# Cosine by way of whole turns: the turns found on VectorE from PSUM, and the quarter turn moved into the sine

## Chip, cores and metric

The kernel runs on one core of one Trainium2 chip. The metric is the device time of one execution in microseconds (us). A core has TensorE (PE: matrix products, into the memory PSUM), VectorE (DVE: elementwise), ScalarE (ACT: elementwise, and functions such as sine and exponential), GpSimd (POOL) and SyncE (SP: issues transfers). Each works through its own queue of instructions in order, and they wait for each other by semaphores.

## What is computed

Attention over a small memory (8 batches, 8 heads, 576 tokens, 64 numbers a head, 32 memory slots), and behind it a layer h -> h cos(h) between two large products:

```python
def _attn_ref(q, k, v, phi):
    a = np.exp(phi - np.max(phi, axis=2, keepdims=True))
    a = a / (np.sum(a, axis=2, keepdims=True) + 1e-09)
    k_m = np.einsum('bhsm,bhsd->bhmd', a, k)
    v_m = np.einsum('bhsm,bhsd->bhmd', a, v)
    scores = np.matmul(q, k_m.transpose(0, 1, 3, 2)) / np.sqrt(q.shape[-1])
    attn = softmax(scores)
    return np.matmul(attn, v_m)

def _moe_ref(x, w_in, w_out):      # x: 4608 x 512, w_in: 512 x 2048, w_out: 2048 x 512
    h = x @ w_in
    g = h * np.cos(h)
    return g @ w_out
```

(Here `softmax` is short for the written-out one of the reference.) The weights come as 64-bit floats.

## The kernel before

The 4608 tokens are taken in 12 **groups** of 384, and the 2048 hidden numbers in 16 chunks of 128; a **step** is one chunk of one group, so there are 192 steps. Two batches of 576 tokens make three groups. The middle one of each three (groups 1, 4, 7 and 10) holds the end of one batch and the start of the next, 192 tokens each, and its steps have two **regions** of 192 columns; all others have one region of 384 (`regions`). Group 0 works in float32, the others with every operand split in two float16 parts.

A step has these parts:

- `gemm1`: TensorE makes the tile `hp` (hidden numbers by tokens) in PSUM. v_m is folded into w_in beforehand (the tiles `vw`, or `vf` in group 0), so the softmaxed scores `aT` are its other operand: 6 matmuls of 384 columns, or 12 of 192 with two regions.
- `act`: `hp` is in a scaled unit, and `cu` (one column of 128 numbers, one for each batch) turns it into turns of the circle. ScalarE writes u = turns + 1/4 (L503, one instruction a region). VectorE converts u to the nearest integer into the space of `gp` (L508) and subtracts it (L509), so that u is within half a turn.
- `act_end`: ScalarE takes the sine of 2 pi u, which is cos(h) (L513). VectorE multiplies it by `hp` (L517); ScalarE makes the first float16 part of the product (L519), VectorE the second (L520), in `gp`. Group 0 has one product in float32 instead (L515).
- `gemm2`: 9 matmuls of 512 columns add the step's part of the outputs to three accumulators (L538; L533 in group 0). It runs four steps behind (`LAG`).

`hp` has three buffers in PSUM, `u` three and `gp` six in SBUF. A buffer of `hp` is free once L517 has read it.

Beside the steps other work is handed in piece by piece. Beside group 0: the weights are converted to float32 (L133 to L142) and folded for the first batch (L456, L458). Beside group 1: both weights are split in two float16 parts (L178, L179 for w_out; L189, L190 for w_in), as are the first batches' folded weights (L439, L440). From there on up to group 9 each next batch is prepared: the softmax over tokens and the sums over them, k_m and v_m, the scores and their softmax (`memory`, `attend`), and the fold of v_m into w_in (`fold`).

The program is written in this order; a scheduler then places the instructions in each engine's queue by priority and by its own estimate of when each one can run. Only where `keep_in_program_order` stands is a place kept. So a change of one instruction's engine can shift others.

Of the kernel before, what the change touches and what calls it, by code (L numbers as in the profile page):

```python
# [11 lines left out]
F32 = mybir.dt.float32  # L12
I16 = mybir.dt.int16
I32 = mybir.dt.int32
# [3 lines left out]
AF = mybir.ActivationFunctionType  # L18
ALU = mybir.AluOpType
# [26 lines left out]
def attention_then_ffn(ctx: ExitStack, tc: tile.TileContext, phi, phiT, kv, qT, w_in, w_out, out):  # L46
# [13 lines left out]
    make_identity(nc, ident)  # L60
    # in X, heads of even number hold [k | v] and those of odd number [v | k]
    vmask = const.tile([P, 2, 2], F32, name="vmask")
# [4 lines left out]
    w_in_sb = const.tile([P, NP, DF], F32, name="w_in_sb")  # L67
    # w_out: block f + 1 holds rows f * 128 on as float32, later block f their two float16 parts
    wo = const.tile([P, NF + 1, DM], F32, name="wo")

    def wo_parts(f):
        return wo[:, f].bitcast(F16).rearrange("p (w e) -> p w e", w=2)

    vl = const.tile([P, NP, 2, M], F16, name="vl")
    nc.vector.memset(vl, 0.0)
# [24 lines left out]

# [1 line left out]
    raws = itertools.count()  # L102
# [4 lines left out]
    def load_w_in(j):  # L107
        if j in (2, 3):
            # the space of w_out's last blocks, which come later
            t = wo[:, 13:17] if j == 2 else wo[:, 9:13]  # L110
            t = t.bitcast(I32).rearrange("p c (f t) -> p c f t", t=2)
        else:
            t = ld.tile([P, NP, WS, 2], I32, tag=next_raw(), name=f"raw_in_{j}")
        nc.sync.dma_start(out=t, in_=w_in[:, 2 * WS * j:2 * WS * (j + 1)].rearrange("(c p) (f t) -> p c f t", p=P, t=2))
        loads["in", j] = t
# [8 lines left out]
    def to_float32(dst, raw, sq_to, pin=False):  # L124
        # the upper half of dst gets the sign, the lower half the last three bits of the mantissa,
        # which lead the low word. The high word as a float32 times 2^-112 has the exponent less
        # 896, three bits too low, and nothing above it.
        low, high = raw[:, :, :, 0], raw[:, :, :, 1]
        flat = raw.rearrange("p c f t -> p c (f t)")
        halves = dst.bitcast(I16).rearrange("p c (f t) -> p c f t", t=2)  # L130
        low_top = flat.bitcast(U8).rearrange("p c (f t) -> p c f t", t=8)[:, :, :, 3]
        high_top = flat.bitcast(I8).rearrange("p c (f t) -> p c f t", t=8)[:, :, :, 7]
        begin = (nc.vector.tensor_scalar(out=halves[:, :, :, 1], in0=high_top, scalar1=0.0, scalar2=-32768.0,  # L133
                                         op0=ALU.is_lt, op1=ALU.mult),
                 nc.scalar.activation(halves[:, :, :, 0], low_top, AF.Copy, scale=2.0 ** -5, bias=-31.0 / 64.0))
        if pin:
            for ins in begin:
                tc.keep_in_program_order(ins)
        nc.scalar.activation(high.bitcast(F32), high.bitcast(F32), AF.Copy, scale=2.0 ** -112)
        nc.vector.scalar_tensor_tensor(out=dst.bitcast(I32), in0=high, scalar=3, in1=dst.bitcast(I32),  # L140
                                       op0=ALU.logical_shift_left, op1=ALU.bitwise_or)
        nc.scalar.activation(low.bitcast(F32), dst, AF.Square, accum_out=sq_to)  # L142
# [6 lines left out]

    # e, a power of two, with every magnitude below 2 e; and 2^14 / e  # L150
    def power_of_two(dst, src):
# [10 lines left out]
    def weight_scale(kind, name):  # L162
        # halving the exponent of the largest sum of squares
        m = const.tile([P, 1], F32, name=f"m_{name}")
        nc.vector.tensor_reduce(out=m, in_=sq[:, kind], op=ALU.max, axis=AX.X)
        nc.gpsimd.partition_all_reduce(m, m, channels=P, reduce_op=RED.max)
        nc.vector.tensor_scalar(out=m, in0=m, scalar1=2.0, scalar2=2.0 ** -100, op0=ALU.mult, op1=ALU.max)
        nc.vector.tensor_scalar(out=m.bitcast(I32), in0=m.bitcast(I32), scalar1=1, scalar2=None,
                                op0=ALU.logical_shift_right)
        nc.vector.tensor_scalar(out=m, in0=m, scalar1=2.0 ** 63, scalar2=None, op0=ALU.mult)  # L170
        e = const.tile([P, 1], F32, name=f"e_{name}")
        power_of_two(e, m)
        st["e", name] = e
        st["s", name] = to_range(f"s_{name}", const, f"s_{name}", e)
# [6 lines left out]

    # w_in in two float16 parts. A head's 64 rows of both parts are brought together on the 128
    # partitions, so that one pass takes both: the first part stays where it is, the second goes to
    # the other half. The slices are kept where a load or an earlier slice was.
    def w_in_split(q, c):
# [17 lines left out]

    # the maximum over the tokens, on all partitions, far ahead of its use
    def maximum(b):
# [7 lines left out]

# [1 line left out]
    def memory(b):  # L215
        a = loads.pop(("phi", b))
        if b < NT:
            # by the tensor engine, from phi transposed
            nmx = wk.tile([P, 2], F32, tag="nmx", name=f"nmx_{b}", bufs=1)
            nc.vector.tensor_reduce(out=nmx, in_=loads.pop(("phiT", b)), op=ALU.max, axis=AX.X)  # L220
            top = small_ps(f"top_{b}")[:, 0:HM]
            for g in range(2):
                nc.tensor.matmul(top[:, g * P:(g + 1) * P], lhsT=nmx[:, g:g + 1].broadcast_to([P, P]), rhs=ident,
                                 start=True, stop=True)
        else:
            top = st["top", b]
# [4 lines left out]
        for c0, c1, n in ((0, 2, P), (2, 4, P), (4, 5, S - 512)) if b == 0 else ((0, 4, P), (4, 5, S - 512)):  # L231
# [3 lines left out]
            if b >= NT:  # L235
                # not sooner: the maximum takes its time
                tc.keep_in_program_order(ins)
# [54 lines left out]

    # the powers of two that bring the two-part float16 operands into range
    def v_scale(b):
# [4 lines left out]
    def scales(b):  # L299
# [10 lines left out]
        else:  # L310
            # the first part of v_m for both parts of w_in, the second part for the first one alone
            sv = to_range(f"sv_{b}", wk, "sv", st["ev", b])
# [9 lines left out]

    # attention over the memory: scores with (head, memory) on the partitions; 32 by 32 blocks are
    # transposed for the softmax over a head's memory, and back
    def attend(b):
        qt, km = loads.pop(("q", b)), st["km", b]
        flat = wk.tile([P, 4 * S], F16, tag="aT", name=f"aT_{b}", bufs=3)
        # the first group works in float32, on the first GT tokens of the first batch
        t32 = GT if b == 0 else 0
# [90 lines left out]

    # v_m folded into w_in
    def fold_psum(b, q, g):
# [46 lines left out]

# [1 line left out]
    def regions(grp):  # L471
# [26 lines left out]

    def act(grp, f, hp, pin=False):
        u = ew.tile([P, GT], F32, tag="u", name=f"u_{grp}_{f}", bufs=3)  # L500
        gp = ew.tile([P, GT], F32, tag="gp", name=f"gp_{grp}_{f}", bufs=6)
        for b, t0, c0, n in regions(grp):
            ins = nc.scalar.activation(u[:, c0:c0 + n], hp[:, c0:c0 + n], AF.Copy,  # L503
                                       scale=st["cu", b] if grp else 1.0 / (2.0 * math.pi), bias=0.25)
            if pin:
                tc.keep_in_program_order(ins)
        ni = gp.bitcast(I32)
        nc.vector.tensor_copy(out=ni, in_=u)  # L508
        nc.vector.tensor_tensor(out=u, in0=u, in1=ni, op=ALU.subtract)  # L509
        return u, gp  # L510

    def act_end(grp, f, hp, u, gp):
        nc.scalar.activation(u, u, AF.Sin, scale=TWO_PI_BELOW)  # L513
        if grp == 0:
# [10 lines left out]
    def gemm2(grp, f, gp):  # L525
        if f == 0:
            # nothing else is left for the small tiles' banks beside the last group
            spare = 2 if grp == 11 else 0
# [11 lines left out]
        if f == NF - 1:  # L540
            # the last group waits for the third accumulator of the one before alone
            for t in (2,) if grp == 10 else range(3):
                evacuate(grp, t)
# [24 lines left out]

# [1 line left out]
    load_phi(0)  # L570
# [31 lines left out]
    fold_first(1)  # L602
    # the other weights, in the order in which they are needed, each a step of the first group
    todo = [("out", 0)]
# [48 lines left out]
    for i in range(12 * NF):  # L653
# [16 lines left out]
        begun.append((grp, f, hp, *act(grp, f, hp, last)))  # L670
        # with nothing else between them, a step's first half goes before the second half of the one before
        while len(begun) > (grp >= 9):
# [66 lines left out]
```

## Time and profile before

| | |
|---|---|
| median of 3 runs | 719.68 us (718.75 to 721.45) |
| span of the profiled execution, first to last instruction | 718.0 us |
| granted TensorE clock, mean over the span | 0.993 |
| TensorE's matmuls L538 (second product) | 1584, 371.3 us busy |
| TensorE's matmuls L494 (first product) | 1440, 202.9 us busy |
| ScalarE's L503, L513, L519 | 118.4 + 99.9 + 89.2 us busy |
| VectorE's L508, L509, L517, L520 | 67.4 + 105.8 + 96.9 + 96.6 us busy |

The profile is of one execution. It has for each instruction its engine, start and length, its line and the tiles that it writes and reads ("u<-hp,cu" writes u and reads hp and cu), and, for idle time, what ended it. An instruction's length runs on until its last result is written, and the next one on the same engine can start a little before. The chain of work that ended last goes back from the last instruction, at each step to what released it. A row of a stretch holds, after its bounds and length, each engine's busy time with the number of its instructions, the granted clock, and the share and rate of the transfers.

### The profile page before, as it was taken

What the parts mean: (1) busy time and instruction counts of PE and PEld (TensorE: products, weight loads), DVE (VectorE), ACT (ScalarE), POOL (GpSimd) and SP (SyncE); (2) the same over time, 40 slices, a digit from 0 to 9 for tenths busy, and PEclk for the clock granted to TensorE, in tenths of its full rate; (3) what the DMA queues carried; (4) which work ended last, traced back from release to release, by engine and by line L of the source; (5) the groups of instructions that cost most, each with busy time, mean ns of one, the idle gap of its engine ahead of it and who ended that gap; (6) DMA issues with size and microseconds to landing.
All of it is one profiled execution on the core that took longest, in us unless ns stands there. A gap on an engine that the chain in (4) does not pass through costs nothing.

```text
span 718.0 us, 12024 instructions
## 1 busy us (share of the span) xinstructions
PE 694.5 (97%) x4578; PEld 357.3 (50%) x4578; DVE 569.6 (79%) x1257; ACT 520.3 (72%) x964; POOL 14.6 (2%) x36
## 2 busy tenths in 40 slices
PE   6689999999999999999999999999999999999997
PEld 2345444565454444565444444566444544555553
DVE  2779999998988997589877897669776987676763
ACT  1699999889886875678756685668767785665553
POOL 0000000000000000000000100000000000000000
PEclk9799999999999999999999999999999999999999
DMA  9994981526405300152104310152100000100101
GB/s 282 382 326 159 310 306 30 132 60 188 148 8 160 110 1 1 45 166 67 45 1 135 96 48 1 45 168 67 44 1 1 22 25 1 45 1 1 45 0 45
DMA packets 31417, 66.72 MB, mean 93 GB/s; under 512 B 2176, under 2 KB 10880, under 8 KB 31360
## 3 DMA queue, kind: packets, MB, share of 16 engines
q1 hardware_dynamic: 27040, 58.09, 25.5%
q10 hardware_dynamic: 4320, 7.87, 2.9%
q8 instruction: 36, 0.59, 0.3%
q14 instruction: 21, 0.17, 0.1%
HBM read 52.31 MB, written 9.44 MB: 86 GB/s over the span
## 4 chain that ended last, share of the span: by engine, by line
PE 59%; DVE 20%; ACT 14%; issue 3%; DMA 3%; POOL 0%; SPq 0%; DVEq 0%; ACTq 0%; POOLq 0%
PE acc L538 34%; PE hp L494 18%; PE pv L433 3%; DVE u L517 3%; DVE gp L520 2%; DVE u L509 2%; DMA phi<-in_phi 2%; ACT u L513 2%; DVE gp L508 2%; ACT L513 1%; DVE vw L440 1%; PE psA L248 1%; ACT raw_out L142 1%; DVE wo L179 1%; PE sc L350 1%
## 5 line engine op out<-in xcount | busy, mean ns | idle before, releaser
L538 PE MATMUL acc<-wo,gp 128*128 128x512 f16 x1584 | 371.3, 379 | 0.0
L538 PEld LDWEIGHTS <-gp 128*128 128x128 f16 x1584 | 153.4, 98 | 161.6 <-issue 2.6
L494 PE MATMUL hp<-aT,vw 128*128 128x192 f16 (+1 forms) x1440 | 202.9, 284 | 1.4 <-DVE u L517 1.2
L494 PEld LDWEIGHTS <-vw 128*128 128x128 f16 x1440 | 125.0, 98 | 84.0 <-issue 30.7
L513 ACT ACTIVATE u<-u 128x384 f32<-128x384 f32 x192 | 99.9, 524 | 88.5 <-DVE u L509 87.4
L517 DVE SCALAR_TENSOR_TENSOR u<-hp,u 128x384 f32<-128x384 f32 x176 | 96.9, 553 | 45.8 <-ACT u L513 43.5
L503 ACT ACTIVATE u<-hp,cu 128x192 f32<-128x192 f32 (+1 forms) x240 | 110.9, 492 | 17.0 <-PE hp L494 10.8
L520 DVE TENSOR_TENSOR gp<-u,gp 128x384 f16<-128x384 f32 x176 | 96.6, 552 | 29.8 <-ACT gp L519 29.3
L519 ACT CAST gp<-u 128x384 f16<-128x384 f32 x176 | 89.2, 509 | 40.0 <-DVE u L517 37.9
L509 DVE TENSOR_TENSOR u<-u,gp 128x384 f32<-128x384 f32 x192 | 105.8, 552 | 3.1
L508 DVE CAST gp<-u 128x384 int32<-128x384 f32 x192 | 67.4, 354 | 20.4 <-ACT u L503 18.7
L533 PE MATMUL acc<-wo,gp 128*128 128x512 f32 x96 | 45.5, 599 | 0.2 <-DVE gp L515 0.2
L440 DVE SCALAR_TENSOR_TENSOR vw<-pv,vw 128x512 f16<-128x512 f32 x48 | 33.1, 689 | 4.7 <-ACT vw L439 3.4
L439 ACT ACTIVATE vw<-pv 128x512 f16<-128x512 f32 x48 | 28.3, 591 | 6.4 <-PE pv L433 5.5
L485 PE MATMUL hp<-aT,vf 128*128 128x384 f32 x64 | 26.4, 545 | 4.2 <-DVE gp L515 2.0
L513 ACT ACT_TABLE_LOAD x23 | 29.5, 1283 | 0.4
L533 PEld LDWEIGHTS acc<-wo,gp 128*128 128x128 f32 x96 | 17.2, 190 | 17.4 <-issue 12.9
L248 PE MATMUL psA<-kv,phi 128*32 128x129 f32 (+1 forms) x640 | 23.5, 277 | 0.8 <-ACT phi L238 0.8
L554 ACT ACTIVATE ob<-acc,os 128x512 f32<-128x512 f32 x28 | 18.5, 683 | 8.0 <-PE acc L538 6.1
L248 PEld LDWEIGHTS psA<-kv,phi 128*32 128x32 f32 (+1 forms) x640 | 16.0, 109 | 11.2 <-issue 5.9
L485 PEld LDWEIGHTS hp<-aT,vf 128*128 128x128 f32 x64 | 12.4, 206 | 17.2 <-issue 5.3
L350 PE MATMUL sc<-q,km 128*64 128x256 f32 (+3 forms) x192 | 20.2, 336 | 0.0
(129 smaller groups left out, 553.3 us busy)
## 6 DMA issues: line engine op xcount, KB each, us to landing
kv<-in_kv SPq DMA_DIRECT2D x32, 516.0 KB, 5.8
q<-in_qT SPq DMA_DIRECT2D x8, 1152.0 KB, 5.7
raw_out<-in_w_out SPq DMA_DIRECT2D x8, 1024.0 KB, 5.5
out<-ob ACTq DMA_DIRECT2D x30, 256.0 KB, 2.1
raw_in<-in_w_in SPq DMA_DIRECT2D x6, 1024.0 KB, 7.3
phi<-in_phi SPq DMA_DIRECT2D x8, 512.0 KB, 6.7
w_in_sb<-w_in_parts SPq DMA_DIRECT2D x12, 256.0 KB, 4.6
phiT<-in_phiT SPq DMA_DIRECT2D x4, 576.0 KB, 8.0
```

The lines of the kernel that those rows point to most:

```text
L248: nc.tensor.matmul(psA[32 * j:32 * (j + 1), g * KV:(g + 1) * KV], lhsT=a[:n, c, h * M:(h + 1) * M], rhs=kvs[c][:n, h * KV:(h + 1) * KV], s ...
L440: nc.vector.scalar_tensor_tensor(out=vw[:, 1, g], in0=src, scalar=T, in1=vw[:, 0, g], op0=ALU.mult, op1=ALU.subtract)
L494: nc.tensor.matmul(hp[:, c0:c0 + n], lhsT=vw[:, wi, g, fo * P:(fo + 1) * P], rhs=aT[:, ai, g, c1:c1 + n], start=(k == 0), stop=(k == 5))
L503: ins = nc.scalar.activation(u[:, c0:c0 + n], hp[:, c0:c0 + n], AF.Copy, scale=st["cu", b] if grp else 1.0 / (2.0 * math.pi), bias=0.25)
L508: nc.vector.tensor_copy(out=ni, in_=u)
L509: nc.vector.tensor_tensor(out=u, in0=u, in1=ni, op=ALU.subtract)
L513: nc.scalar.activation(u, u, AF.Sin, scale=TWO_PI_BELOW)
L517: nc.vector.scalar_tensor_tensor(out=u, in0=hp[:, :GT], scalar=2.0 ** -17, in1=u, op0=ALU.mult, op1=ALU.mult)
L519: nc.scalar.copy(gp[:, 0], u)
L520: nc.vector.tensor_tensor(out=gp[:, 1], in0=u, in1=gp[:, 0], op=ALU.subtract)
L533: nc.tensor.matmul(accs[grp][t], lhsT=gp[:, t * P:(t + 1) * P], rhs=wo[:, f + 1], start=(f == 0), stop=(f == NF - 1))
L538: nc.tensor.matmul(accs[grp][t], lhsT=gp[:, gi, t * P:(t + 1) * P], rhs=parts[:, wi], start=(f == 0 and gi == 0 and wi == 0), stop=(f == N ...
```

## The change

`act` no longer uses ScalarE. VectorE takes `hp` from PSUM, multiplies it by the turns' scale, adds 1/4 and writes the result as integers into `gp`, one tensor_scalar a region. Then one scalar_tensor_tensor a region multiplies `hp` by the same scale and subtracts the integers. What is left is u without its quarter turn, and the sine gets that back as a bias, from a constant column `quarter` that is set once. All else of a step is as before.

```diff
+    quarter = const.tile([P, 1], F32, name="quarter")
+    nc.vector.memset(quarter, TWO_PI_BELOW / 4.0)
...
     def act(grp, f, hp, pin=False):
         u = ew.tile([P, GT], F32, tag="u", name=f"u_{grp}_{f}", bufs=3)
         gp = ew.tile([P, GT], F32, tag="gp", name=f"gp_{grp}_{f}", bufs=6)
+        ni = gp.bitcast(I32)
         for b, t0, c0, n in regions(grp):
-            ins = nc.scalar.activation(u[:, c0:c0 + n], hp[:, c0:c0 + n], AF.Copy,
-                                       scale=st["cu", b] if grp else 1.0 / (2.0 * math.pi), bias=0.25)
+            turns = st["cu", b] if grp else 1.0 / (2.0 * math.pi)
+            ins = nc.vector.tensor_scalar(out=ni[:, c0:c0 + n], in0=hp[:, c0:c0 + n], scalar1=turns, scalar2=0.25,
+                                          op0=ALU.mult, op1=ALU.add)
             if pin:
                 tc.keep_in_program_order(ins)
-        ni = gp.bitcast(I32)
-        nc.vector.tensor_copy(out=ni, in_=u)
-        nc.vector.tensor_tensor(out=u, in0=u, in1=ni, op=ALU.subtract)
+        for b, t0, c0, n in regions(grp):
+            turns = st["cu", b] if grp else 1.0 / (2.0 * math.pi)
+            nc.vector.scalar_tensor_tensor(out=u[:, c0:c0 + n], in0=hp[:, c0:c0 + n], scalar=turns,
+                                           in1=ni[:, c0:c0 + n], op0=ALU.mult, op1=ALU.subtract)
         return u, gp

     def act_end(grp, f, hp, u, gp):
-        nc.scalar.activation(u, u, AF.Sin, scale=TWO_PI_BELOW)
+        nc.scalar.activation(u, u, AF.Sin, scale=TWO_PI_BELOW, bias=quarter)
```

The new lines shift the numbers: in the changed kernel the tensor_scalar is L508 and the scalar_tensor_tensor L514, the sine is L519, the product L523, and the two halves are L525 and L526; the weight splits L179 and L190 are L181 and L192, and L440 is L442. In the rows below a name's first number is the step's chunk, the last one the tile's.

VectorE's queue in group 1, before, from the third step's conversion to the same step's last half:

```order
L508 CAST gp_3_987<-u_3_986 128x384
L509 TENSOR_TENSOR u_3_986<-u_3_986,gp_3_987 128x384
L508 CAST gp_4_1021<-u_4_1020 128x384
L509 TENSOR_TENSOR u_4_1020<-u_4_1020,gp_4_1021 128x384
L517 SCALAR_TENSOR_TENSOR u_3_986<-hp_3_961,u_3_986 128x384
L508 CAST gp_5_1060<-u_5_1059 128x384
L440 SCALAR_TENSOR_TENSOR vw_2_996<-pv_2_1_1078,T_750,vw_2_996 128x512
L520 TENSOR_TENSOR gp_3_987<-u_3_986,gp_3_987 128x384
```

The same queue and step in the changed kernel:

```order
L508 TENSOR_SCALAR gp_3_973<-hp_3_947,cu_702 128x192
L508 TENSOR_SCALAR gp_3_973<-hp_3_947,cu_738 128x192
L526 TENSOR_TENSOR gp_2_926<-u_2_925,gp_2_926 128x384
L514 SCALAR_TENSOR_TENSOR u_3_972<-hp_3_947,cu_702,gp_3_973 128x192
L514 SCALAR_TENSOR_TENSOR u_3_972<-hp_3_947,cu_738,gp_3_973 128x192
L442 SCALAR_TENSOR_TENSOR vw_2_982<-pv_2_0_983,T_740,vw_2_982 128x512
L523 SCALAR_TENSOR_TENSOR u_3_972<-hp_3_947,u_3_972 128x384
L181 SCALAR_TENSOR_TENSOR wo<-wo,s_out 128x512
L526 TENSOR_TENSOR gp_3_973<-u_3_972,gp_3_973 128x384
```

Two instructions of 384 columns have become four of 192. Steps 4 and 5 no longer stand between the third step's parts; the weights' splits and folds do, and they are still in this stage.

ScalarE's queue at the same place, before:

```order
L503 ACTIVATE u_3_986<-hp_3_961,cu_710 128x192
L503 ACTIVATE u_3_986<-hp_3_961,cu_748 128x192
L503 ACTIVATE u_4_1020<-hp_4_1007,cu_710 128x192
L503 ACTIVATE u_4_1020<-hp_4_1007,cu_748 128x192
L503 ACTIVATE u_5_1059<-hp_5_1046,cu_710 128x192
L503 ACTIVATE u_5_1059<-hp_5_1046,cu_748 128x192
L513 ACTIVATE u_3_986<-u_3_986 128x384
```

And in the changed kernel:

```order
L519 ACTIVATE u_3_972<-u_3_972,quarter 128x384
L525 CAST gp_3_973<-u_3_972 128x384
L441 ACTIVATE vw_2_982<-pv_2_1_1064,T_740 128x512
L180 ACTIVATE wo<-wo,s_out 128x512
L191 ACTIVATE w_in_parts_1158<-w_in_sb,s_in 128x512
L519 ACTIVATE u_4_1006<-u_4_1006,quarter 128x384
```

The copies are gone, and the sines stand among the weights' splits.

VectorE's queue in group 11, the last, before:

```order
L508 CAST gp_11_7293<-u_11_7292 128x384
L509 TENSOR_TENSOR u_11_7292<-u_11_7292,gp_11_7293 128x384
L517 SCALAR_TENSOR_TENSOR u_11_7292<-hp_11_7285,u_11_7292 128x384
L520 TENSOR_TENSOR gp_11_7293<-u_11_7292,gp_11_7293 128x384
L508 CAST gp_12_7318<-u_12_7317 128x384
```

And in the changed kernel:

```order
L508 TENSOR_SCALAR gp_11_7172<-hp_11_7164,cu_6135 128x384
L526 TENSOR_TENSOR gp_10_7148<-u_10_7147,gp_10_7148 128x384
L514 SCALAR_TENSOR_TENSOR u_11_7171<-hp_11_7164,cu_6135,gp_11_7172 128x384
L523 SCALAR_TENSOR_TENSOR u_11_7171<-hp_11_7164,u_11_7171 128x384
L508 TENSOR_SCALAR gp_12_7196<-hp_12_7188,cu_6135 128x384
```

The second half of a step now stands behind the next step's tensor_scalar.

## Prediction, made before the changed kernel ran

> **What bounds the kernel now.** I read the head of the page first, for the busy shares, then the chain of work that ended last, stretch by stretch, and then the busy time of the engines in the same stretches.
>
> ```profile
> span 718.0 us, 12024 instructions
> PE 694.5 (97%) x4578; PEld 357.3 (50%) x4578; DVE 569.6 (79%) x1257; ACT 520.3 (72%) x964; POOL 14.6 (2%) x36
> ```
>
> A TensorE that is busy for 97% of the span looks like the one bound, but matmul ends are modelled, and the share is a mean over stages. The chain of a late stretch shows what a step costs when nothing holds it up:
>
> ```profile
> 664.33 1.94 PE acc L538 x9
> 666.27 0.97 PE hp L494 x6
> 667.25 1.94 PE acc L538 x9
> ```
>
> Nine matmuls of the second product (1.94 us) and six of the first (0.97) follow each other without a gap: 2.92 us a step, TensorE alone on the chain. The next two rows are the chain's shares by line in 109 to 167 us (group 1) and in 282 to 338 us (group 4):
>
> ```profile
> by line: DVE wo L179 14.6%; DVE w_in_parts L190 13.6%; DVE vw L440 12.7%; DVE u L509 11.9%; DVE gp L520 10.2%; DVE u L517 10.0%; DVE gp L508 7.3%; DMA w_in<-w_in_parts 6.7%; issue 2.4%; ACT L238 2.2%; ACT raw_out L142 2.1%; ACT u L503 1.8%;
> ...
> by line: PE acc L538 20.8%; PE hp L494 13.0%; DMA phi<-in_phi 12.3%; DVE u L517 4.5%; ACT u L513 3.7%; DVE u L509 3.7%; DVE gp L520 3.5%; PE pv L433 2.9%; DVE gp L508 2.8%; DVE at L352 2.8%; DVE rs L361 2.5%; ACT phi L238 2.4%; DVE rm L356
> ```
>
> In the first stretch the seven VectorE lines make 80% of the chain. In the second TensorE leads. So the kernel has two parts, and the busy times of the stretches say where the border lies. The stretches are, in order: group 0, 1, 2 and 3 of the twelve groups of 16 steps, and group 10:
>
> ```profile
> 32.20:109.30 77.10, 73.68 (x325) 35.38 (x326) 69.93 (x141) 75.44 (x109) 1.59 (x5) 0.96 0.81 273
> 109.30:166.60 57.30, 57.02 (x350) 31.63 (x349) 56.90 (x120) 52.70 (x113) 0.66 (x2) 1.00 0.29 70
> 166.60:226.40 59.80, 58.88 (x458) 29.26 (x457) 51.50 (x123) 50.83 (x84) 0.97 (x3) 1.00 0.46 142
> 226.40:281.80 55.40, 54.96 (x336) 25.59 (x333) 48.90 (x112) 39.58 (x76) 2.06 (x4) 1.00 0.15 46
> 607.20:657.40 50.20, 50.20 (x378) 30.14 (x377) 32.76 (x66) 29.53 (x69) 0.00 (x0) 1.00 0.05 17
> ```
>
> Each row gives the stretch, its length, and the busy time of TensorE, its weight loads, VectorE, ScalarE and GpSimd. In group 0 ScalarE is busy for 75.44 of 77.10 us. In **group 1 VectorE is busy for 56.90 of 57.30 us**: nothing can be added to it there for free. From group 3 on VectorE has some 6 us of room in a group, in group 10 over 17.
>
> **The change, part by part.** It takes one ScalarE copy per region from each step, and the SBUF conversion and subtraction from VectorE. It adds, per region, a tensor_scalar from PSUM to int32 and a scalar_tensor_tensor from PSUM and int32. Steps of groups 1, 4, 7 and 10 have two regions of 192 columns, the others one of 384. The rows of what goes, and of the nearest kin of what comes:
>
> ```profile
> L503 ACT ACTIVATE u<-hp,cu 128x384 f32<-128x384 f32 x112 | 63.8, 576 | 12.4 <-PE hp L494 8.0 <-ACT ob L554 1.7 <-DVE gp L520 0.6
> L503 ACT ACTIVATE u<-hp,cu 128x192 f32<-128x192 f32 x128 | 47.3, 419 | 4.6 <-PE hp L494 2.9 <-ACT ob L554 1.2 <-DVE gp L520 0.2
> L503 ACT ACTIVATE u<-hp 128x384 f32<-128x384 f32 x16 | 7.5, 492 | 0.1
> L508 DVE CAST gp<-u 128x384 int32<-128x384 f32 x192 | 67.4, 354 | 20.4 <-ACT u L503 18.7
> L509 DVE TENSOR_TENSOR u<-u,gp 128x384 f32<-128x384 f32 x192 | 105.8, 552 | 3.1
> L517 DVE SCALAR_TENSOR_TENSOR u<-hp,u 128x384 f32<-128x384 f32 x176 | 96.9, 553 | 45.8 <-ACT u L513 43.5
> L440 DVE SCALAR_TENSOR_TENSOR vw<-pv,vw 128x512 f16<-128x512 f32 x48 | 33.1, 689 | 4.7 <-ACT vw L439 3.4
> L440 DVE SCALAR_TENSOR_TENSOR vw<-pv,T,vw 128x512 f16<-128x512 f32 x8 | 5.9, 744 | 0.1
> L262 DVE TENSOR_SCALAR X<-psA,den 128x128 f32<-128x128 f32 x16 | 5.3, 344 | 0.2
> L552 DVE TENSOR_SCALAR ob<-acc,os 128x512 f32<-128x512 f32 x1 | 0.8, 750 | 3.8 <-PE acc L538 3.8
> ```
>
> *The tensor_scalar.* No row before writes int32 from PSUM. L262 and L552 are tensor_scalars from PSUM with a scalar taken from a column, 344 ns at 128 columns and 750 at 512. That is 406 / 384 = 1.06 ns a column, so 344 + 256 x 1.06 = 615 ns at 384 columns and 412 at 192. The lower bound is the conversion that goes, 354 ns at 384 columns, which reads SBUF and writes the same int32. I take 615, as it reads PSUM. The Trainium skill, "VectorE: DVE Perf Modes", section "Why PSUM operands drop a tier", says that fp32 from PSUM has no doubled mode since PSUM offers VectorE one read port. By it the cheap conversion is lost, and 615 would stand; the trace agrees in that the PSUM rows run at 1.06 ns a column, while 354 ns for 384 columns is less than that.
>
> *The scalar_tensor_tensor.* L517, with PSUM and SBUF inputs, takes 553 ns at 384 columns, and L440 689 at 512: again 1.06 a column, so 553 - 204 = 349 at 192. A scalar from a column costs 744 - 689 = 55 more, so 608 and 404. Group 0 has its scalar in the instruction: 560 and 553.
>
> *What VectorE is held for* is less than a duration, since the next one starts before the end:
>
> ```profile
> 134.24 0.36 DVE L508 CAST gp<-u 128x384 int32<-128x384 f32 x1
> 134.64 0.56 DVE L509 TENSOR_TENSOR u<-u,gp 128x384 f32<-128x384 f32 x1
> 135.11 0.35 DVE L508 CAST gp<-u 128x384 int32<-128x384 f32 x1
> ...
> 136.44 0.35 DVE L508 CAST gp<-u 128x384 int32<-128x384 f32 x1
> 136.71 0.74 DVE L440 SCALAR_TENSOR_TENSOR vw<-pv,T,vw 128x512 f16<-128x512 f32 x1
> ```
>
> The subtraction's 0.56 us hold it for 0.47 (134.64 to 135.11), so 0.09 overlap. The conversion holds it for 0.40 us before its own subtraction and 0.27 before other work. The pair costs 0.74 to 0.87 us, 0.80 in the middle. After the change a two-region step costs 2 x (0.412 - 0.09) + 2 x (0.404 - 0.09) = 1.27 us, **0.47 more** (0.40 to 0.53); the second tensor_scalar fills the first one's wait. A one-region step costs 0.525 + 0.52, with up to 0.1 of wait 1.10, so 0.30 more; in group 0 some 0.16 more.
>
> *Group 1*: 16 x 0.47 = **7.5 us**. VectorE is full there, and the order keeps that stage's other VectorE work (the weight splits L179 and L190, the folds L440) in it. So all of it counts.
>
> *Group 0*: ScalarE loses 14 copies of 0.49 us in the stretch (6.9), and VectorE gains 16 x 0.16 = 2.6, to 72.5 of 77.10. The sine's bias from a column makes each sine longer; by L503 with and without its column that is 576 - 492 = 84 ns, 1.2 us here. With both engines near full, and each waiting for the other, I take **-1 us**, from 0 to -2.9 (72.5 plus the 1.7 us that ScalarE now idles).
>
> *Groups 2 to 9.* A group of one-region steps gets 16 x 0.30 = 4.8 us of VectorE, which fits as a mean: 48.90 + 4.8 in 55.40. It doesn't fit in the bursts in which a batch is prepared:
>
> ```profile
> 240.00:264.00 24.00, 24.00 (x143) 10.92 (x142) 22.90 (x49) 20.35 (x39) 0.00 (x0) 1.00 0.22 82
> 312.00:336.00 24.00, 24.00 (x182) 14.47 (x181) 22.91 (x61) 17.45 (x39) 2.05 (x4) 1.00 0.33 107
> 408.00:432.00 24.00, 24.00 (x129) 11.61 (x128) 23.25 (x52) 20.86 (x36) 0.25 (x1) 1.00 0.27 83
> ```
>
> Each stretch of 24 us has some 7 steps, so 7 x 0.30 = 2.1 us more (7 x 0.47 = 3.3 in the second, which is in group 4): 25.0, 26.2 and 25.3 against 24.0, an excess of 4.5 us. The steps in hand (three product tiles, and four steps between the two products) take up part, so I count **3.7 us**, from 0 to 4.5.
>
> *Groups 10 and 11*: nothing. VectorE goes from 32.76 to at most 41 of 50.20. At the end the chain of a step on VectorE (tensor_scalar, last step's subtraction of halves, scalar_tensor_tensor, sine, product) is about 2.9 us, as long as TensorE's 2.92; should it lag, 54 matmuls of the second product stand ready behind it:
>
> ```profile
> 702.25 11.67 PE acc L538 x54
> ```
>
> *The rest*: the column of quarter turns is one small memset early on. The copies gone, the sines' table loads fall by two and the exponentials' by two in the order, on ScalarE only, which has room from group 2 on. Buffers keep their lives: the product tile was held until L517 reads it, and still is. The DMA queue of SyncE has the same transfers; a few of k and v come sooner among the weights' loads, which I cost at nothing, as no load is on the chain of groups 0 and 1 but the 3.89 us of w_in's parts.
>
> *Sum*: 718.0 - 1 + 7.5 + 3.7 = 728.2 us of span. The median of the runs is 719.68, 1.7 above the span, so 729.9: **730 us, 1.4% slower**.
>
> **The rivals.** *Spare time absorbs it (not slower).* Over groups 0 to 2 VectorE is busy for 69.93 + 56.90 + 51.50 = 178.3 of 194.2 us and gets 2.6 + 7.5 + 4.8 = 14.9, to 193.2. Were it never idle, with ScalarE relieved, group 2 would win back what group 1 loses; TensorE isn't on top in group 2 either. The mechanism decides if group 2 shrinks from 59.8 to about 54. With the bursts hidden too, and group 0 at -2.9, that gives 717 to 720, and 715 if ScalarE's relief takes 2 us more from group 2. Against it: the order leaves group 1's VectorE work in group 1, and group 2 itself gets 4.8 us more. Chance 0.18 (0.05 faster, 0.13 the same).
>
> *VectorE becomes the bound in every preparing stage (slower still).* Groups 2 to 9 get 6 x 4.8 + 2 x 7.5 = 43.8 us. Were it to count in the half of the steps beside which a batch is prepared, that is 22 us in place of 3.7, so 748. For it: VectorE now also waits for the sine right behind its own work in each step. Against it: TensorE leads there, with several us of VectorE free. Chance 0.13.
>
> *The int32 comes out of PSUM as quickly as out of SBUF.* Then group 1 adds 16 x (0.95 - 0.80) = 2.4 us, the bursts nothing: 721. Chance 0.07 (0.05 the same, 0.02 slower). By the skill's rule above it can't be; that sentence changes nothing in the 0.07, which comes from the missing row.
>
> **How the numbers follow.** My forecast gets 0.57, and lies between 724 and 742. A new order that gains or loses elsewhere keeps 0.05 (0.03 faster, 0.02 slower). About 0.5% is what a measurement of this kernel can tell from no change. Faster by over that: 0.05 + 0.03 = 0.08. The same: 0.13 + 0.05 = 0.18. Slower: 0.57 + 0.13 + 0.02 + 0.02 = 0.74. The range goes from 717 to 748: it leaves out the lower part of the first rival and the upper half of the second.
>
> **What would show it.** Right: tensor_scalars of about 412 and 615 ns, scalar_tensor_tensors of 404 and 608; group 1 some 65 us long with VectorE over 98% busy; ScalarE's busy time down by 63.8 + 47.3 + 7.5 less 192 x 0.084, about 102 us; group 10 as long as before. Wrong: group 1 under 60 us, or groups 3 to 9 longer by over 2 us each, or group 0 shorter by over 3.

## The result: 1.55% slower, and the profile after

| | before | after |
|---|---|---|
| median | 719.21 us | 730.76 us |
| ratio, 95% interval | | 1.0155 [1.0137, 1.0173] |
| span of the profiled execution | 718.0 us | 728.0 us |

A second time, on another chip, the changed kernel took 730.74 us against 720.61: 1.0136 [1.0114, 1.0159].

The head of the changed kernel's page:

```profile
span 728.0 us, 11891 instructions
PE 695.7 (96%) x4578; PEld 358.6 (49%) x4578; DVE 631.0 (87%) x1385; ACT 432.3 (59%) x705; POOL 13.5 (2%) x36
```

VectorE has 61.4 us more, ScalarE 88.0 less, TensorE about the same (1.2 more). The groups of instructions that are new, and the sine with its bias (line, engine, shapes, count, then busy time and the mean in ns):

```profile
L514 DVE SCALAR_TENSOR_TENSOR u<-hp,cu,gp 128x384 f32<-128x384 f32 x112 | 68.0, 609 | 0.7
L508 DVE TENSOR_SCALAR gp<-hp,cu 128x384 int32<-128x384 f32 x112 | 67.4, 604 | 3.7 <-PE hp L496 3.4
L508 DVE TENSOR_SCALAR gp<-hp,cu 128x192 int32<-128x192 f32 x128 | 48.0, 408 | 4.9 <-PE hp L496 4.5
L514 DVE SCALAR_TENSOR_TENSOR u<-hp,cu,gp 128x192 f32<-128x192 f32 x128 | 47.2, 407 | 0.0
L508 DVE TENSOR_SCALAR gp<-hp 128x384 int32<-128x384 f32 x16 | 8.7, 550 | 2.2 <-PE hp L487 2.2
...
L519 ACT ACTIVATE u<-u,quarter 128x384 f32<-128x384 f32 x192 | 116.9, 613 | 172.0 <-DVE u L514 155.4 <-DVE l L286 6.4 <-DVE ev L154 3.9
```

Where the 10 us lie is seen by group. These are the changed kernel's stretches for groups 0, 1, 2 and 3, and group 10, with the columns as before (bounds, length, busy TensorE, weight loads, VectorE, ScalarE, GpSimd, granted clock, share and rate of the transfers):

```profile
32.40:112.40 80.00, 76.11 (x324) 35.74 (x324) 71.64 (x139) 74.22 (x99) 1.64 (x5) 0.94 0.74 252
112.40:177.40 65.00, 58.40 (x355) 32.18 (x355) 64.01 (x145) 44.10 (x75) 0.66 (x2) 1.00 0.24 61
177.40:237.30 59.90, 56.88 (x451) 29.59 (x450) 58.13 (x128) 39.77 (x64) 0.98 (x3) 1.00 0.45 143
237.30:292.80 55.50, 55.09 (x337) 25.66 (x334) 52.22 (x113) 32.93 (x58) 2.07 (x4) 1.00 0.17 56
617.20:667.40 50.20, 50.20 (x377) 30.13 (x376) 41.28 (x102) 22.70 (x41) 0.00 (x0) 1.00 0.05 17
```

Group 1 is 7.7 us longer by these rows (57.30 to 65.00), group 0 2.9 (77.10 to 80.00), and groups 2, 3 and 10 are as long as before within 0.3. In group 1 VectorE is busy for 64.01 of 65.00 us, and ScalarE's busy time has fallen from 52.70 to 44.10 without any use. What TensorE waited for in group 1 of the changed kernel (what waited, for whom, us in total, times, the longest):

```profile
PE hp L496 <- DVE u L523: 6.0, 6, 1.9
```

A matmul of the first product needs a free buffer of `hp`, and VectorE's product L523 frees it. Before the change this wait was 0.3 us in all.

By group 3 the changed kernel is some 11 us late, so the stretches of 24 us that had been called full lie 10 or 11 us later in it. The first and the third:

```profile
250.00:274.00 24.00, 24.00 (x144) 10.92 (x142) 23.64 (x53) 18.29 (x30) 0.10 (x1) 1.00 0.24 83
...
419.00:443.00 24.00, 23.50 (x126) 11.40 (x125) 23.82 (x50) 17.09 (x26) 0.31 (x1) 1.00 0.26 78
```

There VectorE is busy for 98% and more (97% in the second stretch), and TensorE lost half a us in the third alone. Groups 2 to 9 together are no longer than before: 439.8 us against 440.6.

### The profile page after: what moved, and what is told of

The parts are those of the page before. It is cut to its first block, busy times and chain, and to the rows that moved or that the text cites. A ratio compares the mean times of both kernels' runs of the same rounds, so it can differ in the third digit from the quotient of the medians.

```text
span 728.0 us, 11891 instructions
## 1 busy us (share of the span) xinstructions
PE 695.7 (96%) x4578; PEld 358.6 (49%) x4578; DVE 631.0 (87%) x1385; ACT 432.3 (59%) x705; POOL 13.5 (2%) x36
## 4 chain that ended last, share of the span: by engine, by line
PE 62%; DVE 22%; ACT 9%; issue 3%; DMA 3%; POOL 0%; SPq 0%; ACTq 0%; POOLq 0%
PE acc L544 32%; PE hp L496 17%; PE pv L435 3%; DVE gp L508 3%; DVE u L514 3%; DVE u L523 3%; DVE gp L526 2%; PE psA L250 2%; PE hp L487 2%; PE acc L539 2%; PE sc L352 2%; ACT u L519 1%; DVE w_in_parts L192 1%; DVE wo L181 1%; DMA w_in_sb<-w_in_parts 1%
## 5 line engine op out<-in xcount | busy, mean ns | idle before, releaser
L519 ACT ACTIVATE u<-u,quarter 128x384 f32<-128x384 f32 x192 | 116.9, 613 | 172.0 <-DVE u L514 155.4
L523 DVE SCALAR_TENSOR_TENSOR u<-hp,u 128x384 f32<-128x384 f32 x176 | 96.3, 551 | 37.1 <-ACT u L519 36.2
L525 ACT CAST gp<-u 128x384 f16<-128x384 f32 x176 | 88.1, 508 | 61.1 <-DVE u L523 56.7
L508 DVE TENSOR_SCALAR gp<-hp,cu 128x192 int32<-128x192 f32 (+1 forms) x240 | 115.4, 499 | 8.6 <-PE hp L496 8.0
L514 DVE SCALAR_TENSOR_TENSOR u<-hp,cu,gp 128x192 f32<-128x192 f32 (+1 forms) x240 | 115.2, 501 | 0.7
L526 DVE TENSOR_TENSOR gp<-u,gp 128x384 f16<-128x384 f32 x176 | 96.1, 552 | 4.4 <-ACT gp L525 2.2
L442 DVE SCALAR_TENSOR_TENSOR vw<-pv,vw 128x512 f16<-128x512 f32 x48 | 33.0, 687 | 4.9 <-ACT vw L441 4.7
```

The source lines that it names most:

```text
L508: ins = nc.vector.tensor_scalar(out=ni[:, c0:c0 + n], in0=hp[:, c0:c0 + n], scalar1=turns, scalar2=0.25, op0=ALU.mult, op1=ALU.add)
L514: nc.vector.scalar_tensor_tensor(out=u[:, c0:c0 + n], in0=hp[:, c0:c0 + n], scalar=turns, in1=ni[:, c0:c0 + n], op0=ALU.mult, op1=ALU.subt ...
L519: nc.scalar.activation(u, u, AF.Sin, scale=TWO_PI_BELOW, bias=quarter)
L523: nc.vector.scalar_tensor_tensor(out=u, in0=hp[:, :GT], scalar=2.0 ** -17, in1=u, op0=ALU.mult, op1=ALU.mult)
L525: nc.scalar.copy(gp[:, 0], u)
L526: nc.vector.tensor_tensor(out=gp[:, 1], in0=u, in1=gp[:, 0], op=ALU.subtract)
```

## The experiments

The theory: the loss is VectorE's added time in group 1, which has no room for it. Rivals: the new order of the queues (with the transfers of w_in's parts, which have 11.9% of the changed kernel's chain in group 1, against 6.7% before), or the longer way of one tile through VectorE, or a cost in all groups that a gain elsewhere covers. The experiments choose by group which way the turns are found (`act_by_copy` is the old `act`, word for word).

### The new way in some groups alone

```diff
+NEW = (0, 2, 3, 4, 5, 6, 7, 8, 9, 10, 11)
...
     def act(grp, f, hp, pin=False):
+        if grp not in NEW:
+            return act_by_copy(grp, f, hp, pin)
...
-        nc.scalar.activation(u, u, AF.Sin, scale=TWO_PI_BELOW, bias=quarter)
+        nc.scalar.activation(u, u, AF.Sin, scale=TWO_PI_BELOW, **({"bias": quarter} if grp in NEW else {}))
```

That is g1_old; the others differ in `NEW` alone. What was expected of group 1 old; of groups 0 and 1 old; of group 0 alone new; and of group 1 alone new:

> The changed kernel, but group 1 finds its turns as before (copy on ScalarE, conversion and subtraction from SBUF, sine without bias). Theory: VectorE is full in group 1, and the whole of that group's 7.6 us is the added VectorE time, so group 1 goes from 65.0 back to 57 to 59 us and the span from 728.0 to about 720.5. Rival: the new order of the queues, with w_in's parts on the chain, made group 1 longer; then it stays above 62 us and the span above 725.

> The changed kernel, but groups 0 and 1 find their turns as before. Theory: what the change costs lies in these two groups alone, and the ten others hide theirs, so the span is 717 to 719 and the time that of the kernel before. Rival: the other groups' added VectorE time costs something that a gain elsewhere now covers; then the span is above 721.

> The kernel before, but group 0 finds its turns by the new way. Theory: the 3.0 us that group 0 lost come from its own added VectorE time and the order that follows from it, so group 0 is 79 to 81 us and the span about 721. Rival: group 0 lost them because work of group 1 is handed in earlier or later; then group 0 is about 77 us and the span 718. If the relief of ScalarE is worth something, group 0 is 75 us or less.

> The kernel before, but group 1 alone finds its turns by the new way. Theory: 16 steps of 0.47 us more on a full VectorE: group 1 is 64 to 66 us and the span 725 to 726. Rival: the loss needs the new way in the groups beside it too; then group 1 is below 61 us and the span below 722.

Then, on one chip, the changed kernel again, group 0 old, and groups 0 and 1 alone new:

> The changed kernel once more, on the chip of the next three kernels. Expected by every theory: 1.3 to 1.7% over the kernel before, with group 1 at 65 us. What is open is group 0, which took 77.1 us before and 80.1 in the changed kernel's profile: a granted clock of one half that comes at another moment each run (then 77 to 81 us by chance), or the change (then 80 again).

> The changed kernel, but group 0 finds its turns as before. If group 0 lost its 3.0 us by the change, this is 3 us below the changed kernel on the same chip, some 1.1% over the kernel before. If it lost them by the clock, the two agree within 1 us.

> The kernel before, but groups 0 and 1 find their turns by the new way. If groups 2 to 11 hide theirs, this is as slow as the changed kernel within 1 us. If they cost the 3.7 us that were predicted for them, it is 3 to 4 us below it.

Measured (length of a group from its first matmul of `gemm1` to the next group's):

| kernel | new way in | ratio to before, 95% | group 0 | group 1 | group 2 |
|---|---|---|---|---|---|
| before | none | | 77.1 | 57.4 | 59.7 |
| changed | all | 1.0155 [1.0137, 1.0173] | 80.1 | 65.0 | 60.0 |
| after_again | all | 1.0136 [1.0114, 1.0159] | 80.1 | 65.0 | 60.0 |
| g1_old | all but 1 | 0.9994 [0.9977, 1.0011] | 80.4 | 56.8 | 58.5 |
| g01_old | 2 to 11 | 0.9998 [0.9974, 1.0022] | 76.9 | 57.4 | 59.5 |
| g0_new | 0 | 1.0026 [1.0001, 1.0050] | 77.5 | 56.8 | 59.3 |
| g1_new | 1 | 1.0092 [1.0074, 1.0111] | 77.0 | 65.1 | 58.3 |
| g0_old | 1 to 11 | 1.0083 [1.0058, 1.0109] | 77.1 | 65.1 | 58.1 |
| g01_new | 0, 1 | 1.0120 [1.0100, 1.0140] | 79.1 | 65.0 | 59.2 |

Group 1 is 65.0 or 65.1 us wherever it has the new way, and 56.8 or 57.4 wherever it hasn't, whatever the groups beside it do. Groups 2 to 11 cost nothing: g01_old agrees with before. g01_new is 0.16% (1.2 us) below the changed kernel run with it, within the intervals of both, where the predicted 3.7 us would have been 0.5%.

### Group 0: the change or the clock

Group 0 is less plain: 77.5, 79.1, 80.1 or 80.4 us with the new way, and some 77 without. g0_new was expected at 79 to 81 and came out where its rival had put it. The granted clock differs too. Stretches of group 0, first from three kernels with the new way in it (g0_new, g01_new, g1_old), then from two without (stt_alone_g1, which is told of below, and g0_old); the clock is the third number from the right:

```profile
32.90:110.40 77.50, 73.21 (x325) 34.86 (x326) 72.03 (x142) 74.49 (x99) 1.84 (x6) 0.98 0.75 256
```
```profile
33.80:112.90 79.10, 75.28 (x324) 35.62 (x325) 71.73 (x140) 74.21 (x99) 1.63 (x5) 0.95 0.72 248
```
```profile
32.80:113.20 80.40, 76.44 (x325) 36.20 (x326) 72.14 (x142) 74.53 (x99) 1.82 (x6) 0.93 0.74 250
```
```profile
32.10:107.90 75.80, 72.09 (x325) 34.83 (x326) 69.84 (x141) 75.26 (x109) 1.60 (x5) 0.98 0.82 277
```
```profile
33.00:110.10 77.10, 74.05 (x324) 35.22 (x324) 69.97 (x141) 75.37 (x109) 1.60 (x5) 0.95 0.80 267
```

At a clock of 0.98 the new way takes 77.50 us and the old one 75.80; at 0.95 it is 79.10 and 77.10. By these two pairs of profiles the change costs group 0 **1.7 to 2.0 us**, and the rest of its 3.0 in the profile goes with the clock (0.94 against 0.96). A part of the cost can be seen: TensorE's longest wait in group 0, for VectorE's product that frees `hp`, is 3.0 to 3.2 us in the kernels with the new way there (3.2 in g0_new, 3.1 in g01_new) and 2.0 in those without (before, g0_old and stt_alone_g1 among them).

The timed runs agree less well. g0_new is +0.26% [0.01, 0.50], 1.9 us; the changed kernel is 0.53%, 3.8 us, above g0_old, where 3 us had been expected of the change and under 1 of the clock; yet g1_old, with the new way in group 0, is as fast as g01_old without it (0.9994 and 0.9998). So the timed runs put the cost between nothing and 4 us; some 2 us is an estimate from the pairs of profiles.

The clock doesn't visibly follow the change. In stretches of 4 us of group 0 it lies between 0.50 and 1.00, so its loss can be told as time at half clock, (1 - clock) x 2 x span. That is on average 16.9 us in the 25 timed runs of before beside g1_old, and 17.1 and 17.2 in the two sets of the changed kernel. In the other kernels, one_more aside, it lies between 1.4 us below and 3.1 above the kernel before on the same chip with the new way in group 0, and between 0.9 below and 2.6 above without it.

### Each half of the change alone, in group 1

ts_alone_g1: only the conversion reads PSUM, and ScalarE's copies stay.

```diff
         for b, t0, c0, n in regions(grp):
+            ins = nc.vector.tensor_scalar(out=ni[:, c0:c0 + n], in0=hp[:, c0:c0 + n], scalar1=st["cu", b], scalar2=0.25,
+                                          op0=ALU.mult, op1=ALU.add)
             nc.scalar.activation(u[:, c0:c0 + n], hp[:, c0:c0 + n], AF.Copy, scale=st["cu", b], bias=0.25)
-        nc.vector.tensor_copy(out=ni, in_=u)
         nc.vector.tensor_tensor(out=u, in0=u, in1=ni, op=ALU.subtract)
```

> The kernel before, but in group 1 the conversion alone is done from PSUM (two tensor_scalars of 192 columns in place of the 384-column conversion from SBUF); ScalarE's copies stay and feed the subtraction. By the price list a step holds VectorE for 2 x 0.32 + 0.47 = 1.11 us instead of 0.80: group 1 is 5 us longer, 62 to 63 us. If what counts is that ScalarE and VectorE now work one after the other, not VectorE's time, group 1 stays at 57 to 59.

stt_alone_g1: only the subtraction reads PSUM, and the sine has its bias.

```diff
         nc.vector.tensor_copy(out=ni, in_=u)
-        nc.vector.tensor_tensor(out=u, in0=u, in1=ni, op=ALU.subtract)
+        for b, t0, c0, n in regions(grp):
+            nc.vector.scalar_tensor_tensor(out=u[:, c0:c0 + n], in0=hp[:, c0:c0 + n], scalar=st["cu", b],
+                                           in1=ni[:, c0:c0 + n], op0=ALU.mult, op1=ALU.subtract)
```

> The kernel before, but in group 1 the subtraction alone is done from PSUM (two scalar_tensor_tensors of 192 columns, and the sine's bias); ScalarE's copies and the conversion from SBUF stay. By the price list a step holds VectorE for 0.34 + 2 x 0.31 = 0.96 us instead of 0.80: group 1 is 2.6 us longer (1.6 to 3.6), 59 to 61 us. The two halves then make up the whole of 7.6. If there is another cause than VectorE's time, the halves don't add up.

Measured: 1.0057 [1.0029, 1.0086] and 1.0047 [1.0022, 1.0072]. Group 1's stretch in each, ts_alone_g1 first:

```profile
110.20:173.30 63.10, 58.96 (x359) 32.45 (x358) 62.54 (x134) 54.05 (x110) 0.66 (x2) 1.00 0.27 68
```
```profile
107.90:169.10 61.20, 57.76 (x351) 33.01 (x350) 60.57 (x135) 55.16 (x114) 0.66 (x2) 0.97 0.26 67
```

VectorE is busy for 62.54 of 63.10 and 60.57 of 61.20 us, as it was for 56.90 of 57.30 before and 64.01 of 65.00 after: the stage is VectorE's busy time and 0.4 to 1.0 us, at four different amounts. By the stretches both halves came out above their expectation (5.8 us against 5.0, and 3.9 against 2.6), and add up to more than the whole (9.7 against 7.7). By the timed runs there is no such excess: 0.57% and 0.47% are 4.1 and 3.4 us, 7.5 together, against 6.6 (0.92%) for the whole in g1_new, each within some 2 us. In ts_alone_g1 group 2 is 57.7 us, 2.0 below the kernel before, and the second row's clock of 0.97 is part of its 61.20; so a stretch alone doesn't settle whether the halves add up.

### VectorE's work taken out of group 1

```diff
     def w_in_split(q, c):
...
-        nc.vector.scalar_tensor_tensor(out=parts[:, 1, c], in0=src, scalar=s, in1=parts[:, 0, c],
-                                       op0=ALU.mult, op1=ALU.subtract)
+        nc.gpsimd.memset(parts[:, 1, c], 0.0)
```

after_less is the changed kernel with this, before_less the kernel before with it.

> The changed kernel, but the second float16 parts of w_in are left out (zeros, written by GpSimd, in place of VectorE's 16 subtractions of 128x512 in group 1), so the output lacks that share. It takes 16 x 0.66 = 10.6 us from VectorE in group 1. If VectorE's time is what makes group 1 65 us long, it falls to 56 to 58 us, where TensorE's own work ends it, and the span to about 720. If the longer way from the product tile to the sine is what counts, group 1 stays above 62.

> The kernel before, with the second float16 parts of w_in left out in the same way. If VectorE alone set group 1 before the change, it falls from 57.4 us by several us. If TensorE was as near its end there, as the forecast of 7.5 us for the whole addition implies, group 1 stays at 55 to 57.4 us.

Measured: 1.0035 [1.0017, 1.0052] and 0.9999 [0.9981, 1.0017], both against the full kernel before. Group 1's stretch, after_less first:

```profile
112.40:170.10 57.70, 57.37 (x354) 31.88 (x354) 53.89 (x129) 43.22 (x75) 5.89 (x14) 1.00 0.36 87
```
```profile
109.10:165.90 56.80, 56.02 (x351) 31.62 (x350) 54.13 (x114) 53.07 (x113) 7.00 (x14) 1.00 0.35 85
```

With 16 of VectorE's instructions fewer the changed kernel's group 1 is back at 57.70 us, though each tile takes the new way to its sine. So it is VectorE's amount of work that counts, not the way of one tile. Nor is it the transfers of w_in's parts: they are still made, and have 18.9% of the chain in after_less's group 1. The kernel before gets nothing for the same work less: there VectorE and TensorE end the stage together, near 57 us. What is left is after_less's 0.35%, 2.5 us, about group 0's share.

### How far the room of groups 3 to 9 goes

```diff
+        if 3 <= grp <= 9:
+            spare = ew.tile([P, GT], I8, tag="spare", name=f"spare_{grp}_{f}", bufs=1)
+            nc.vector.tensor_scalar(out=spare, in0=hp[:, :GT], scalar1=0.5, scalar2=0.25, op0=ALU.mult, op1=ALU.add)
         return u, gp
```

> The changed kernel with one more instruction on VectorE in each step of groups 3 to 9, which nothing waits for: a tensor_scalar of 384 columns from PSUM into a spare tile, some 0.47 us of VectorE a step, 7.5 a group. It asks where the room ends. If room counts as a mean over a group, groups 3, 6 and 9 (52.2, 50.6 and 49.0 us busy of 55.5, 52.9 and 50.8) grow by 4 to 6 us each, groups 4 and 7 by 1, groups 5 and 8 by nothing: 14 to 20 us in all. If the bursts set it, as the prediction had it, every preparing group grows, and the sum is over 25 us.

Measured: 1.0420 [1.0395, 1.0445], 750.62 us, 19.9 above the changed kernel on the same chip. The sum is just inside the first expectation, but its places are not:

```profile
239.10:295.10 56.00, 55.70 (x342) 26.36 (x339) 55.04 (x119) 32.02 (x56) 2.07 (x4) 1.00 0.17 56
295.10:352.00 56.90, 56.78 (x487) 34.10 (x486) 54.18 (x137) 27.26 (x48) 1.91 (x3) 1.00 0.27 88
352.00:414.70 62.70, 55.34 (x371) 26.05 (x369) 59.41 (x126) 34.40 (x60) 0.31 (x1) 0.95 0.14 47
```

Group 3, in the first row, had no room for 7.5 us by its mean, and grows by half a us. Group 5, in the third, had the most, and grows by 8.5. Group 8 does the same. Taken over groups 3 to 5, VectorE was busy in the changed kernel for this long (the sum line of those three stretches):

```profile
sum 165.80, PE 165.23 PEld 85.04 DVE 148.86 ACT 95.50 POOL 4.12; mean PE 55.08 PEld 28.35 DVE 49.62 ACT 31.83 POOL 1.37
```

That leaves 16.9 us. The 48 added instructions hold it for 48 x 0.46 = 22.1, 5.2 too many, and the three groups grow by 175.6 - 165.8 = 9.8. Groups 3 and 4, with VectorE busy for 55.04 of 56.00 and 54.18 of 56.90 us, lose little; in group 5 TensorE waits 5.9 us for VectorE's product. So the room is neither that of a 24-us burst nor of one group: work that finds VectorE full is done later, and here the debt fell due in the third group. Only this one load was tried, so how long a smaller debt may run isn't shown. The third row's clock of 0.95 is part of the 9.8: TensorE was busy for only 1.93 us from 363 to 369 us, and from 369 to 375 the granted clock was 0.50.

## Why the prediction was right, and where it was right by luck

The predicted 730 us met 730.76, and the span of 728.2 the profile's 728.0. Term by term:

| term | predicted | measured |
|---|---|---|
| group 1 | +7.5 | +7.7 in the profile; 57 against 65 us in the kernels of the table above |
| group 0 | -1 (0 to -2.9) | +2.9 in the profile; +1.7 to +2.0 at equal clock; 0 to 4 by the timed runs |
| bursts in groups 2 to 9 | +3.7 (0 to 4.5) | nothing (-0.8 in the profile) |
| groups 10 and 11 | 0 | 0 |

**Group 1 was right in place, cause and size.** The tensor_scalars take 604 and 408 ns (615 and 412 were worked out) and the scalar_tensor_tensors 609 and 407 (608 and 404). VectorE's busy time is 98% of the stage. Taking the work away brought the stage back, and half of it costs about half.

**Group 0 was wrong in sign.** The step that failed is the one by which ScalarE's relief outweighs VectorE's addition, since ScalarE was the busier engine. ScalarE's busy time there fell by 1.2 us only (75.44 to 74.22), where the copies less the longer sines were to give 5.7. The sum took ScalarE's instructions at their whole durations, where for VectorE the prediction had taken off what two of them overlap. The durations of ScalarE's instructions that start in group 0 add up to 4.9 us less (87.0 to 82.1), but there were 11.5 us of overlap among them before and 7.7 after. In the whole kernel the same step shows: the copies' 118.6 us went and the sines took 17.0 more, as forecast, but ScalarE's busy time fell by 88.0, not 102. The scheduler also gave ScalarE one more of the stage's free copies (4 of L460 against 3). VectorE went up by 1.7 (69.93 to 71.64), and TensorE's wait for it by some 1 us. Both engines stayed over 89% busy, and the gain on one wasn't collected. What costs the rest of the 1.7 to 2.0 us isn't shown.

**The bursts were wrong in mechanism.** The step that failed is the sum over stretches of 24 us. VectorE's debt is carried on, in one_more up to the third group, so an excess of 1 us in 24 waits for the next quiet stretch. The range's lower end of nothing was the right one. The two errors, 3.9 us in group 0 with its clock and 3.7 in the bursts, nearly cancel in the total: its closeness owes as much to that luck as to the method.

**The rivals.** The first asked group 2 to pay back what group 1 loses; it decides if group 2 shrinks to about 54. Group 2 stayed at 60.0 in the changed kernel. It shrank to 58.1 in g0_old and 58.3 in g1_new, but also to 58.5 in g1_old, where group 1 had lost nothing; so a payback isn't shown, and one of 1 to 2 us would be far from enough. The second, VectorE as the bound in every preparing stage, didn't come true: even with one instruction more a step (one_more), groups 5 and 8 alone grow by over 2 us. The third fell with the durations: from PSUM the conversion to int32 takes 604 ns at 384 columns, and 550 where its scale is no column, against 354 from SBUF before. The Trainium skill, "VectorE: DVE Perf Modes", section "Why PSUM operands drop a tier", says that fp32 from PSUM has no doubled mode; the 604 and the 550 ns agree with that.

No version beats the kernel before: the best mixtures, g1_old and g01_old, agree with it within 0.3%. From group 3 on TensorE sets the time with either way, and in group 1 of the kernel before it is within 1 us of doing so.

## What to carry to other kernels

Price an edit stage by stage: 88 us less on one engine and 61 more on another made some 2 us of difference in eleven of twelve groups together, and 7.7 us in the one group where the receiving engine had no idle time. Where a stage is as long as one engine's busy time, a duration that moves there is paid in full. Where an engine has room, ask over how long a time its debt may be carried (here up to the third group) before calling a short burst a loss, and don't book a gain on a relieved engine while its partner is as full.

## What the runs showed of the hardware that had not been expected

The granted TensorE clock in group 0 differs between runs of like kernels (0.93 to 0.98 over some 78 us), and that group's length differs with it by up to 3 us, as much as the edit under test. It was told apart as far as it could be by comparing groups of equal clock; whether a lower clock made the group longer, or a wait in it lowered the clock, isn't shown there. In the changed kernel's profile the clock is 1.00 in every group from 1 on, but it was 0.97 in group 1 of stt_alone_g1. Where VectorE was overloaded and TensorE waited (one_more, groups 5 and 8), it was 0.95, so there an overload is paid a little more than once.
